# A shorter lead of the row maxima over the exponentials: 28 half-turns instead of 30

## The chip, the cores and the metric

The kernel runs on one core of a Trainium2 chip. Its time is device microseconds (us) for one execution; the times before are 1682.55, 1682.76 and 1683.22 us, median 1682.76. The engines are PE (the matrix multiplier, with its weight loads PEld), DVE (vector), ACT (scalar functions), POOL (general purpose) and SP, which here only issues DMAs. Each works through its own instructions strictly in the order in which they were written; they meet at semaphores.

## The reference

One transformer block with adaptive layer norm, 2048 tokens of width 512, 32 query heads of width 16 that share one key and one value head, and a bilinear gated layer of width 1792. Cut to what matters:

```python
mod = (_silu(c) @ w_mod).reshape(c.shape[0], 6, 1, -1)
sa, ca, ga, sb, cb, gb = (mod[:, 0], mod[:, 1], ..., mod[:, 5])
h = _layernorm(x) * (1 + ca) + sa
q, k, v = h @ wq, h @ wk, h @ wv                  # 32 heads of q, one of k and v
p = softmax(q @ k.T * 16 ** -0.5)                 # per head, 2048 x 2048
x = x + ga * ((p @ v) @ wo)
h = _layernorm(x) * (1 + cb) + sb
x = x + gb * (((h @ w_gate) * (h @ w_up)) @ w_down)
```

## The kernel before

**Units, turns, half-turns.** The tokens of q are cut in 4 blocks of 512, the heads in 8 groups of 4; a block with a group is a *unit*, 32 in all, and a unit has 16 *turns*, one for each 128 keys. For each turn PE computes four score tiles (tile `sc`, line 621, 128 keys by 512 queries), ACT takes their exponentials (tile `P`, line 623), and PE multiplies the exponentials of the turn before with the values (tile `pv`, line 632).

**Maxima.** The softmax needs the maximum of every score row first. So all scores are computed twice: once with queries on the partitions (tile `mx`, line 570), where DVE reduces each tile of 512 keys to its maximum (`mpart`, line 574), and once for the exponentials. A unit has 32 maxima steps (the first has 24), each with one tile in the upper half of PE's rows and one in the lower (`a` = 0 and 1). When the last step of a unit is done, DVE folds the partial maxima into `mm` (line 591). PE then transposes `mm` (tile `mxt`, line 598), ACT and DVE split the result into two half-precision rows (`mt`, lines 603 and 604), and two DMAs from SP put them into rows 48 and 49 of the query tile `sst` (line 608). The score matmul of that unit contracts over 50 rows, so it subtracts the maxima itself; it can start only when both DMAs have landed. Three `sst` tiles take turns.

**Order.** All instructions are written out by hand in program order; no scheduler moves them. First comes a *lead* of `LEAD` rounds, in which only maxima steps run, with the last of the preparation beside them: the modulation rows (`misc`, line 868, four matmuls for each of four rounds, then a copy and transposes) from round `M_STEP` on, and the first q product, in bursts of two or three matmuls (`Q_BURSTS`, tile `side`, line 485). After it, each turn writes two half-turns of maxima and two of exponentials, so the maxima stay `LEAD` half-turns ahead, until they run out.

**Side work.** Between them stands the work of the other layers (`side`, line 485): q products for later blocks (a store of q, line 518, goes out through SP), output projection, gate, up and down products. Two turns form an `attend`. With q products as side work its string is `FEW`, with the other products `MANY`, with none `NO_SIDE`. In `FEW` and `MANY` the maxima of the upper rows stand in the first turn and those of the lower rows in the second; `NO_SIDE` alternates.

**Where the row maxima are handed over.** A finished unit leaves its transposes under the step at which they may be written, one maxima step after the last. `late_max` looks for them in the middle of a turn and at its end. It writes the transposes and leaves the copies and DMAs for the next `drain_posts`, which stands at the start of a turn and in its middle, there just ahead of `late_max`:

```python
if last:
    max_fin(u)
    (_, f, g), = max_rows(u)
    later[mstep[1] + 1] = (f, g)      # f: transposes, g: copies and DMAs
...
drain_posts()
for j, (what, a) in enumerate(order):
    if j == len(order) // 2:
        drain_posts()
        late_max()
```

At the end of a unit the maxima's counter `mstep`, the exponentials and the lead thus decide together in which turn transposes, copies and DMAs fall.

Of the kernel before, what the change touches and what calls it, by code (L numbers as in the profile page):

```python
# [24 lines left out]
NU = NB * UB  # L25
KT = S // 128
FT = F // 128
LEAD = 30
WARM = (21, 3, 2, 3)
ABS_GAP = 2.5  # L30
SUM_GAP = 7.0
# [2 lines left out]
QPRE = 24  # L34
TR_WAIT = 11
NHF = 12
M_STEP = 23
PAIRED = 14
Q_BURSTS = {26: 3, 27: 3, 28: 3, 29: 2}

CHANNEL = {0: KC - 1, 3: 0, 4: 1, 6: 2}
LOW = -3.0e38
# [12 lines left out]
def adaln_mqa_glu_kernel(ctx: ExitStack, tc: tile.TileContext, x_in, wq_in, wk_in, wv_in, wo_in,  # L55
# [453 lines left out]
    def q_proj(b, ch):  # L509

        def evac(p):
            q16 = work.tile([128, 2, BT], F16, name="q16", tag="ev", bufs=3)
            qf = work.tile([128, BT], F32, name="qf", tag="ev", bufs=3)
            nc.scalar.activation(qf, p, AF.Copy, scale=qvs[:, 0:1])
            nc.gpsimd.tensor_scalar(q16[:, 0, :], qf, 1.0, 0.0, op0=OP.mult, op1=OP.add)
            nc.gpsimd.tensor_tensor(q16[:, 1, :], qf, q16[:, 0, :], op=OP.subtract)
            d = dram.tile([128, 2, BT], F16, name=f"qd{b}_{ch}")
            nc.sync.dma_start(d, q16)
            qd[b, ch] = d

        def op(i):
            k, term = divmod(i, 3)
            wl, hl = TERMS[term]
            return wq[:, wl, k, ch * 128:(ch + 1) * 128], h16[:, hl, k, b * BT:(b + 1) * BT]

        return Group(3 * KC, op, evac)
# [511 lines left out]
    def drain_posts():  # L1038
        todo = posts[:]
        posts.clear()  # L1040
        if tick[0] is not None:
            tick[0] += 1
            todo += timers.pop(tick[0], [])
        for f in todo:
            f()
# [56 lines left out]
    qs = deque(q_proj(b, ch) for b in range(NB) for ch in range(KC) if b + ch)  # L1102
    for n in range(LEAD):
        drain_posts()
# [5 lines left out]
        if n in first:  # L1110
            first[n]()
        for _ in range(Q_BURSTS.get(n, 0)):
            qs[0].whole()
        if 0 <= n - M_STEP < len(mod_rows):
            mod_rows[n - M_STEP]()
    cur.append(qs[0])
# [163 lines left out]
```

## Time and profile before

| what | value |
|---|---|
| median of 3 runs | 1682.76 us |
| profiled execution, its own time | 1682.67 us |
| span of that execution, first to last instruction | 1680.6 us |
| busy: PE, DVE, ACT, POOL | 1656.3, 1390.0, 1216.1, 518.1 us |
| lead, until the first score tile starts | 74.38 us |
| units 0 to 5, with q products beside them | 74.38 to 323.73 us |
| units 6 to 8, with no side work for most of the time | 323.73 to 446.54 us |
| units 11 to 30, output, gate, up and down products beside them | 539.35 to 1468.36 us |
| last unit, and the products that are left over | 1468.36 to 1680.6 us |

A line of the profile names the engine, the line of the code and the operation, then the tile written and, behind the arrow, the tiles read. In the rows of a stretch of time the first two numbers are start and length in us, "x4" says that four such instructions in a row are put together, and a bracket gives the idle time of the engine before it and who ended it. PE's times are modelled: matmuls follow each other every 0.21 us though each is shown with 0.38 us. SPq is the issue of a DMA, not its transfer.

### The profile page before, as it was taken

Reading aid. Unit: us, or ns where it says so; the run is one execution under the profiler, and the core shown is the slowest. Engines: PE = TensorE matmul, PEld = TensorE weight load, DVE = VectorE, ACT = ScalarE, POOL = GpSimd, SP = SyncE. Lnnn points to the kernel's source line nnn. Section 1 sums busy time; section 2 is a strip of 40 time slices with the busy share of each in tenths; the row PEclk is TensorE's granted clock in tenths of the full one; section 3 lists DMA queues with packets and bytes.
Section 4 is the critical chain, followed back from the end, with each engine's and each line's share of the span. In section 5 each row is a group of like instructions: output and inputs, shape, how many; then the busy total and the mean of one; then the engine's idle time right before and its main releaser. Section 6 shows DMA issues by size and latency. Waiting matters only on the chain.

```text
span 1680.6 us, 33352 instructions
## 1 busy us (share of the span) xinstructions
PE 1656.3 (99%) x12749; PEld 535.4 (32%) x12749; DVE 1390.0 (83%) x2365; ACT 1216.1 (72%) x2288; POOL 518.1 (31%) x690
## 2 busy tenths in 40 slices
PE   8999999999999999999999999999999999999999
PEld 3333333222223333333333333333333333334444
DVE  7999999999989999999989999999998999703110
ACT  5688888888787778777777777877777777772010
POOL 5745354626676740200140211101032111112230
PEclk9999999999999999999999999999999999999999
DMA  6112122211321200001100000000010000001000
GB/s 245 72 40 88 54 88 61 94 48 50 84 66 56 85 22 9 17 10 29 35 15 12 15 15 10 16 10 17 24 32 12 23 16 6 12 5 49 13 1 25
DMA packets 48556, 66.33 MB, mean 39 GB/s; under 512 B 14726, under 2 KB 29194, under 8 KB 48396
## 3 DMA queue, kind: packets, MB, share of 16 engines
q1 hardware_dynamic: 46812, 63.87, 12.2%
q8 instruction: 100, 1.64, 0.4%
q14 instruction: 60, 0.49, 0.1%
q10 hardware_dynamic: 1584, 0.33, 0.1%
HBM read 51.05 MB, written 8.65 MB: 36 GB/s over the span
## 4 chain that ended last, share of the span: by engine, by line
PE 87%; DVE 9%; ACT 2%; DMA 1%; issue 0%; ACTq 0%; DVEq 0%
PE side L485 50%; PE pv L632 27%; DVE mpart L574 8%; PE sc L621 5%; PE mx L570 3%; ACT P L623 2%; PE mx L765 1%; DMA xbig<-in_A_x_dram 1%; PE mxt L598 0%; DVE bs L238 0%; PE sc L570 0%; PE pk L274 0%; DMA wkv<-in_A_wv_dram 0%; DVE rel L579 0%; PE part L267 0%
## 5 line engine op out<-in xcount | busy, mean ns | idle before, releaser
L574 DVE TENSOR_REDUCE mpart<-mx 128x1 f32<-128x512 f32 x2016 | 1266.1, 683 | 91.6 <-PE mx L570 88.3
L623 ACT ACTIVATE P<-sc 128x512 f32<-128x512 f32 x2048 | 1092.0, 599 | 264.6 <-PE sc L621 223.1
L621 PE MATMUL sc<-sst,kst 50*128 50x512 f16 x2048 | 661.0, 379 | 1.0 <-DVE mpart L574 0.8
L570 PE MATMUL mx<-kst,sst 48*128 48x512 f16 x2032 | 617.3, 377 | 6.5 <-DVE mpart L574 3.8
L632 PE MATMUL pv<-P,vst 128*32 128x512 f32 x4096 | 545.3, 605 | 1.2
L485 PE MATMUL side<-h2T,wg 64*128 64x512 f16 (+1 forms) x1168 | 284.3, 378 | 0.1
L485 PE MATMUL side<-h2T,wu 64*128 64x512 f16 (+1 forms) x1166 | 282.9, 378 | 0.1
L485 PE MATMUL side<-wd,glu 64*128 64x512 f16 (+1 forms) x1008 | 234.1, 378 | 0.0
L818 POOL TENSOR_SCALAR glu<-gf 128x512 f16<-128x512 f32 x56 | 34.7, 620 | 617.2 <-DVE gf L817 538.9
L621 PEld LDWEIGHTS <-kst 50*128 50x128 f16 x2048 | 175.2, 94 | 129.4 <-issue 109.6
L570 PEld LDWEIGHTS <-sst 48*128 48x128 f16 x2064 | 183.9, 94 | 58.7 <-issue 37.4
L485 PEld LDWEIGHTS <-wg 64*128 64x128 f16 (+1 forms) x1168 | 100.9, 94 | 202.7 <-ACT P L623 95.0
L485 PEld LDWEIGHTS <-wu 64*128 64x128 f16 (+1 forms) x1166 | 100.8, 95 | 200.2 <-ACT P L623 92.5
L632 PEld LDWEIGHTS pv<-P,vst 128*32 128x32 f32 x4096 | 80.8, 108 | 218.8 <-issue 202.8
L485 PEld LDWEIGHTS <-glu 64*128 64x128 f16 (+1 forms) x1008 | 89.1, 95 | 163.2 <-ACT P L623 63.0
L817 DVE TENSOR_TENSOR gf<-side,g 128x512 f32<-128x512 f32 x56 | 38.3, 684 | 115.8 <-PE side L485 82.5
L485 PE MATMUL side<-h,wq 64*128 64x512 f16 (+1 forms) x349 | 92.5, 376 | 0.0
L812 ACT ACTIVATE g<-side 128x512 f32<-128x512 f32 x56 | 33.2, 593 | 81.5 <-PE side L485 81.5
L485 PE MATMUL side<-wo,och 64*128 64x512 f16 (+1 forms) x336 | 79.3, 378 | 0.0
L819 POOL TENSOR_TENSOR glu<-gf,glu 128x512 f16<-128x512 f32 x56 | 65.0, 1161 | 4.7
L200 POOL TENSOR_SCALAR rv<-st 128x1 f32<-128x1 f32 (+1 forms) x20 | 4.6, 228 | 158.3 <-DVE st L725 143.2
L666 POOL TENSOR_TENSOR oc<-oc,rr 128x512 f32<-128x512 f32 x15 | 19.1, 1275 | 107.4 <-DMA sst<-qd 94.3
(223 smaller groups left out, 810.5 us busy)
## 6 DMA issues: line engine op xcount, KB each, us to landing
wsl<-in_B_w_gate_dram SPq DMA_DIRECT2D x32, 224.0 KB
wsl<-in_B_w_up_dram SPq DMA_DIRECT2D x32, 224.0 KB
wsl<-in_B_w_down_dram SPq DMA_DIRECT2D x28, 256.0 KB
sst<-qd SPq DMA_DIRECT2D x180, 32.0 KB
oc<-ev SPq DMA_DIRECT2D x128, 32.0 KB
rr<-ri SPq DMA_DIRECT2D x16, 256.0 KB
xl<-in_A_x_dram SPq DMA_DIRECT2D x16, 256.0 KB
qd<-q SPq DMA_DIRECT2D x15, 256.0 KB
```

What stands on the lines that cost most here:

```text
L485: return nc.tensor.matmul(self.p, left[64 * r0:64 * r1], right[64 * r0:64 * r1], start=start, stop=self.ended())
L570: nc.tensor.matmul(m, s[64 * a:64 * a + 48, p, t * 128:(t + 1) * 128], w[64 * a:64 * a + 48, :], start=(i == 0), stop=(i == len(keys) - 1))
L574: nc.vector.tensor_reduce(part, m, axis=AX.X, op=OP.max)
L621: nc.tensor.matmul(t, kst[64 * a:64 * a + 50, kt * 128:(kt + 1) * 128], s[64 * a:64 * a + 50, p, :], start=True, stop=True)
L623: ex = nc.scalar.activation(ptl[u, kt, p, a], t, AF.Exp)
L632: nc.tensor.matmul(pvb[u][32 * j:32 * j + 32, :], vst[:, kt, :], ptl[u, kt, p, a], start=(kt == 0), stop=(kt == KT - 1))
L666: eng.tensor_tensor(o, o, st["r"], op=OP.mult)
L765: nc.tensor.transpose(st["p"][:, t * 128:(t + 1) * 128], n2s[b, t][:, k * 128:(k + 1) * 128], ident)
L812: nc.scalar.activation(st["g", f], p, AF.Copy, scale=2.0 ** -45)
L817: nc.vector.tensor_tensor(gf, p, st["g", f], op=OP.mult)
L818: nc.gpsimd.tensor_scalar(st["glu"][:, 0, f, :], gf, 1.0, 0.0, op0=OP.mult, op1=OP.add)
L819: nc.gpsimd.tensor_tensor(st["glu"][:, 1, f, :], gf, st["glu"][:, 0, f, :], op=OP.subtract)
```

## The change

Three numbers: the lead has 28 rounds; the modulation rows start in round 21 and the bursts of the first q product in round 24, so that both end with the lead as before. No instruction's work is changed.

```diff
-LEAD = 30
+LEAD = 28
 ...
-M_STEP = 23
+M_STEP = 21
 PAIRED = 14
-Q_BURSTS = {26: 3, 27: 3, 28: 3, 29: 2}
+Q_BURSTS = {24: 3, 25: 3, 26: 3, 27: 2}
```

From round 14 on a round of the lead is one maxima step. So four `mx` tiles of unit 1 leave the lead, every later maxima step stands two half-turns later against the exponentials, and the last ones of unit 31 stand where side work stood.

The first place is ACT at the beginning of unit 16. `mt` is the first copy of the row maxima, `P` the exponentials (of unit 15 ahead of `mt`), `ev` the copy of unit 15's result, which marks the second turn of unit 16. Before:

```order
L623 ACTIVATE P<-sc 128x512 x8
L812 ACTIVATE g<-side 128x512
L623 ACTIVATE P<-sc 128x512 x40
L603 ACTIVATE mt_11690<-mxt 16x128
L623 ACTIVATE P<-sc 128x512 x16
L638 ACTIVATE ev<-pv,evs 128x512
```

After, at the same place:

```order
L623 ACTIVATE P<-sc 128x512 x8
L812 ACTIVATE g<-side 128x512
L623 ACTIVATE P<-sc 128x512 x48
L603 ACTIVATE mt_11758<-mxt 16x128
L623 ACTIVATE P<-sc 128x512 x8
L638 ACTIVATE ev<-pv,evs 128x512
```

The first copy moves behind eight more exponentials: of the 16 that stood between it and `ev`, eight were unit 15's last two turns; now unit 16's own follow it at once. It is so in 27 of the units 1 to 31. In four (6, 7, 8 and 10, which begin without side work) it moves behind four, and one turn of the old unit is left between.

The second place is SP ahead of unit 2. `qd` is a store of q, `wsl` a load of a weight slice, `sst<-mt` the two rows of maxima. Before:

```order
L897 DMA wsl<-in_B_w_gate_dram 128x448 x3
L608 DMA sst_128<-mt_2213 2x8x128
L608 DMA sst_128<-mt_2214 2x8x128
L897 DMA wsl<-in_B_w_gate_dram 128x448
L518 DMA qd_2_2297<-q_2292 128x1024
L897 DMA wsl<-in_B_w_gate_dram 128x448
```

After:

```order
L518 DMA qd_1_2029<-q_2024 128x1024
L897 DMA wsl<-in_B_w_gate_dram 128x448
L535 DMA sst_126<-qd_1_1039 16x2x512 x6
L897 DMA wsl<-in_B_w_gate_dram 128x448 x3
L518 DMA qd_2_2279<-q_2274 128x1024
L608 DMA sst_128<-mt_2285 2x8x128
L608 DMA sst_128<-mt_2286 2x8x128
```

The rows of maxima moved behind a load and behind the store of q. The same happens ahead of unit 5.

The third place is PE in the lead, at the first of the modulation rows. `mx` and `sc` from line 570 are maxima steps of unit 0 (sst_126) and unit 1 (sst_127). Before:

```order
L570 MATMUL mx<-kst,sst_126 128x512
L868 MATMUL misc<-wmB,silr 32x512 x2
L868 MATMUL misc<-wmA,silr 32x512
L868 MATMUL misc<-wmB,silr 32x512
L570 LDWEIGHTS sst_127
L570 MATMUL mx<-kst,sst_127 128x512
```

After:

```order
L868 MATMUL misc<-wmB,silr 32x512 x2
L868 MATMUL misc<-wmA,silr 32x512
L868 MATMUL misc<-wmB,silr 32x512
L570 LDWEIGHTS sst_126
L570 MATMUL mx<-kst,sst_126 128x512
L570 LDWEIGHTS sst_126
L570 MATMUL sc<-kwb,sst_126 128x512
L570 LDWEIGHTS sst_126
L570 MATMUL sc<-kst,sst_126 128x512
```

The first two groups of modulation matmuls now stand among unit 0's last maxima steps, which have three matmuls for each half; before, all four stood behind them.

## Prediction, made before the changed kernel was run

> **What bounds the kernel now.** I read the page's busy shares and its chain of waits first, then busy time by stretch, then single rows at the end of a unit.
>
> ```profile
> PE 1656.3 (99%) x12749; PEld 535.4 (32%) x12749; DVE 1390.0 (83%) x2365; ACT 1216.1 (72%) x2288; POOL 518.1 (31%) x690
> PE 87%; DVE 9%; ACT 2%; DMA 1%; issue 0%; ACTq 0%; DVEq 0%
> 158.13:323.73 165.60, 164.42 (x1309) 50.01 (x1307) 160.85 (x274) 140.49 (x274) 83.57 (x84) 1.00 0.24 75
> 323.73:446.54 122.81, 116.34 (x855) 30.23 (x852) 121.78 (x219) 102.25 (x199) 61.31 (x79) 1.00 0.20 59
> 539.35:1468.36 929.01, 928.03 (x7703) 286.69 (x7700) 844.75 (x1386) 730.38 (x1363) 179.58 (x215) 1.00 0.07 20
> ```
>
> The stretches give length, then busy PE, PEld, DVE, ACT, POOL, then the granted clock. PE is never idle for long in the units with gate, up and down products (928.03 of 929.01 us), PE and DVE nearly together limit those with q products, DVE (121.78 of 122.81) those without side work. So whatever stops PE between units is lost: in the first kind PE has no slack, and in the others DVE's next maxima stand behind the same scores in PE's order. The execution profiled took 1682.67 us (span 1680.6), 0.09 under the median; I add to 1682.67.
>
> **The hand-over of the row maxima.** Here is the start of unit 16 before; its first score tile starts at 769.87.
>
> ```profile
> 763.20 0.22 DVE L591 TENSOR_REDUCE mm<-mpart 128x16 f32<-128x64 f32 x1
> 763.99 0.28 PE L598 MATMUL mxt<-ident,mm 128*16 128x128 f32 x1
> 764.30 0.27 ACT L603 ACTIVATE mt<-mxt 16x128 f16<-16x128 f32 x1 [0.52 <-PE mxt L598]
> 764.60 0.28 DVE L604 SCALAR_TENSOR_TENSOR mt<-mxt,mt 16x128 f16<-16x128 f32 x1
> 764.59 1.22 SPq L608 DMA_DIRECT2D sst<-mt  x2
> 767.03 0.39 PE L621 MATMUL sc<-sst,kst 50*128 50x512 f16 x1
> 767.46 2.19 ACT L623 ACTIVATE P<-sc 128x512 f32<-128x512 f32 x4 [0.64 <-PE sc L621]
> 767.68 2.56 DVE L574 TENSOR_REDUCE mpart<-mx 128x1 f32<-128x512 f32 x4 [0.30 <-PE mx L570]
> 769.87 0.39 PE L621 MATMUL sc<-sst,kst 50*128 50x512 f16 x1
> 770.38 2.08 ACT L623 ACTIVATE P<-sc 128x512 f32<-128x512 f32 x4 [0.73 <-PE sc L621]
> ```
>
> A turn is 2.84 us (767.03 to 769.87). The second DMA has been issued by 765.81, 4.06 us ahead of the score, and the score waits for nothing. With a lead of 28 the last maxima step of the lower rows falls on the last place of its turn instead of the second. The transposes are allowed one step later; in `FEW` and `MANY` the next turn holds steps of the upper rows alone, so they come in the middle of the turn after that, the old unit's last, and the copies at the very start of the new unit, just ahead of its scores. The order of ACT above shows it. What was two turns ahead is now none.
>
> How long PE then stands, in times from the first score's place s = 769.87: ACT finishes the old unit's exponentials at 767.46 + 2.19 = s − 0.22 and the first copy at s + 0.05; its DMA occupies SP to s + 0.7. DVE finishes the reductions queued ahead at 767.68 + 2.56 = s + 0.37 and the second copy at s + 0.65. Both paths let SP issue the second DMA at about s + 0.7. Its landing is not shown by a row of its own; the nearest rows are DMAs whose reader waits on SP:
>
> ```profile
> L608 SPq DMA_DIRECT2D sst<-mt x64: 508/544/652, 68.1 to 1463.7; - x64
> L647 SPq DMA_DIRECT2D rs<-ev x32: 528/550/555, 124.7 to 1517.9; - x32
> SPq L654 <- DMA rs<-ev: 12.4, 12, 1.2
> L659 SPq DMA_DIRECT2D ri<-rc x16: 325/326/344, 215.1 to 1521.8; - x16
> SPq L661 <- DMA ri<-rc: 18.3, 16, 2.0
> ```
>
> Issue plus mean wait is 0.55 + 12.4/12 = 1.58 us for 8 KB and 0.33 + 18.3/16 = 1.47 for 16 KB. The first has the same issue time as ours (0.54), so I take 1.6; the ends are 1.4 and 2.3 (0.33 + the longest wait). The score starts at s + 0.7 + 1.6: **a wait of 2.3 us** where there was none, between 2.0 and 3.0. The transposes' own 0.2 us of PE only move from one turn to another.
>
> Counted from ACT's order, 27 of 31 hand-overs are of this kind: 27 × 2.3 = 62.1 us. Unit 31 has no maxima beside it, so its second copy comes earlier, but the first DMA's issue still holds SP to s + 0.7; I leave it at 2.3. Something more stands ahead of the copies in several:
>
> ```profile
> 110.32 0.71 ACT L514 ACTIVATE qf<-side,qvs 128x512 f32<-128x512 f32 x1
> 111.14 0.27 ACT L603 ACTIVATE mt<-mxt 16x128 f16<-16x128 f32 x1
> 113.00 0.34 SPq L518 DMA_DIRECT2D qd<-q  x1
> 113.44 1.15 SPq L608 DMA_DIRECT2D sst<-mt  x2
> 154.35 0.34 SPq L897 DMA_DIRECT2D wsl<-in_B_w_gate_dram  x1
> 158.13 0.39 PE L621 MATMUL sc<-sst,kst 50*128 50x512 f16 x1
> 160.31 0.33 SPq L518 DMA_DIRECT2D qd<-q  x1
> 283.99 0.39 PE L621 MATMUL sc<-sst,kst 50*128 50x512 f16 x1
> 285.98 0.35 SPq L518 DMA_DIRECT2D qd<-q  x1
> L812 ACT ACTIVATE g<-side 128x512 f32<-128x512 f32 x56 | 33.2, 593 | 81.5 <-PE side L485 81.5
> L817 DVE TENSOR_TENSOR gf<-side,g 128x512 f32<-128x512 f32 x56 | 38.3, 684 | 115.8 <-PE side L485 82.5
> ```
>
> Ahead of unit 1 the row was copied by 111.41 and its DMA left only at 113.44, behind a store of q that waited for POOL: SP's order counts. Before units 2 and 5 that store now stands ahead of the DMAs, and it is ready only 2.2 and 2.0 us after their scores' old place. Two issues (1.2) and 1.6 us after its own 0.3 they land at s + 5.1: 2.8 us more, twice, 5.6. In units 13, 21, 24 and 29 ACT has one more copy of a side tile ahead (line 812, 0.6 each), in 17 and 27 DVE one more result of the size of line 817's (0.7 each): 3.8. The weight load that moved ahead of unit 2's rows was issued at 154.35, 3.8 us before s, and costs nothing; the single loads and stores that moved ahead elsewhere were issued over 1.4 us before the score too, but for an output store of unit 27, whose result is counted. In the four hand-overs without side work (6, 7, 8, 10) one turn of some 2.4 us remains: the same chain ends about 0.1 to 0.3 after s, with DVE still behind PE; I take 0.6 for the four, between 0 and 2. Sum of the waits: 62.1 + 5.6 + 3.8 + 0.6 = **72.1 us**.
>
> **The lead.** Two rounds with four reductions leave it.
>
> ```profile
> 67.27 2.47 DVE L574 TENSOR_REDUCE mpart<-mx 128x1 f32<-128x512 f32 x4
> 68.02 0.62 PE L868 MATMUL misc<-wmB,silr 128*32 128x512 f32 x2
> 70.09 0.62 PE L868 MATMUL misc<-wmB,silr 128*32 128x512 f32 x2
> 74.38 0.39 PE L621 MATMUL sc<-sst,kst 50*128 50x512 f16 x1
> ```
>
> Four reductions are 2.47 us of DVE: the most the lead can gain. But PE is the limit where modulation rows and bursts meet, 2.07 us a round (68.02 to 70.09), and all of these stay; two groups now meet three matmuls a half instead of one and push PE past DVE there (1.6 us a round against 1.2 by the spacing of the rows, 0.4 each). And unit 0's rows lose the two rounds that covered their landing. I take −1.3, between −2.5 and +0.5. The modulation weights have landed by then (the share of DMA, the last number but one, is 0.00 in the stretch from 50.19 below), so starting sooner waits for nothing. At the end four half-height maxima tiles stand where side tiles stood, which follow later as two whole matmuls: +0.4. Without an effect on the clock: 1682.67 + 72.1 − 1.3 + 0.4 = 1753.9 us.
>
> **The clock.** PE's granted clock fell once within the work:
>
> ```profile
> 42.20 1.12 PE L274 MATMUL pk<-part,selk 128*128 128x512 f32 x2 [1.38 <-ACT part L269]
> 54.80 0.58 PE L570 MATMUL sc<-kst,sst 48*128 48x512 f16 x1 [2.06 <-DVE kst L289]
> 50.19:53.60 3.41, 2.54 (x17) 1.28 (x16) 3.35 (x7) 2.43 (x5) 3.24 (x5) 1.00 0.00 0
> 53.60:57.01 3.41, 2.21 (x12) 0.96 (x13) 3.41 (x6) 1.31 (x3) 3.24 (x5) 0.50 0.00 0
> 57.01:60.43 3.42, 3.42 (x20) 1.62 (x18) 3.42 (x12) 2.84 (x6) 3.25 (x5) 0.50 0.00 0
> ```
>
> The wait that ended at 54.80, the longest of PE after its start, was followed by half the clock for 6.83 us, which is two stretches of 3.41; waits up to 1.38 kept it. The new waits of 2.3 us and more are longer than the one that lost it, so I expect some of them to lose it too, by how they lie on a grid of 3.41 us. I take half of 27, 14. Each then runs a stretch of 3.41 at half speed where PE is the limit: 1.5 us lost, 21 in all, so **1775 us**. The ends are none (1754) and all, with both stretches lost as in the row (27 × 3.2 = 86, 1840).
>
> [...]
>
> **The rivals.**
> - Waits without the clock: 1745 to 1760, likeliest 1754. For it: units without side work, where DVE holds PE up in every turn, kept 1.00. Against: the row at 53.60. Chance 0.27.
> - Both stretches lost after most waits: over 1800. For it: the one case seen did so. Against: its first stretch still held 1.2 us of that wait, ours hold less. Chance 0.08.
> - The waits partly absorbed: only units where PE is the limit pay (22 × 2.3 less 1), or PE's turn, which has 2.69 us of work in its 2.84 (eight pairs of 0.213 and 0.99 of `pv` by the spacing of starts), catches up some of it: 1690 to 1745. Against: PE and DVE both stand idle behind the score. Chance 0.08.
> - Not slower: the rows still land before the score. It decides at a chain of 2.3 us that would have to start one turn sooner, as it does where there is no side work; then the waits fall to about 0 and 1682.67 − 1.3 + 0.4 = 1681.8 is left, no change that a measurement of this kernel can tell (that bound is 0.2%, 3.4 us); even the whole 2.5 us of the lead would not pass it. Against: ACT's order puts the copy right ahead of unit 16's own exponentials. Chance 0.03.
>
> **How the numbers follow.** Waits with some clock lost, 1760 to 1800, has 0.54 and gives 1775. The range 1745 to 1800 takes in this and the first rival, 0.81 in all, and so the ends of the landing time (27 × −0.3 to +0.7). Faster 0.01, within the bound 0.03, slower 0.96.
>
> **What would show it.** In the new profile the first score tile of a unit has an idle PE of 2 to 2.5 us ahead of it, ended by the DMA of the rows, some 5 us for units 2 and 5, and next to none for 6, 7, 8 and 10. The rows' copies stand within 1 us of it. The lead ends at about 73 us. The mean granted clock falls from 0.998 to about 0.985 (14 × 3.41 at half of 1775) if the clock falls at half of the hand-overs. I would be wrong if the DMA landed much sooner than 1.6 us after issue, or if the clock went after every wait or after none.

## The result, and the profile after

The changed kernel takes 1775.59 us, median of four runs (1773.6 to 1777.47), against 1682.66 for the kernel before (four runs, 1682.55 to 1683.22). The ratio is 1.0549, with an interval of 1.0537 to 1.0561: slower by 93 us, where 92 were forecast. The profiled execution took 1773.6 us with a span of 1771.8.

From the page after: the busy shares, the chain of waits, and the group of the score tiles (busy time, mean ns, idle time before them):

```profile
PE 1688.7 (95%) x12747; PEld 539.7 (30%) x12747; DVE 1392.5 (79%) x2365; ACT 1214.8 (69%) x2288; POOL 518.0 (29%) x690
PE 84%; DVE 9%; ACT 3%; DMA 3%; issue 1%; SPq 1%; POOL 0%; ACTq 0%
L621 PE MATMUL sc<-sst,kst 50*128 50x512 f16 x2048 | 667.7, 382 | 61.4 <-DMA sst<-mt 60.0
```

From the list of waits after (us in total, times, longest):

```profile
PE sc L621 <- DMA sst<-mt: 60.0, 28, 4.8
```

And the span with the mean granted clock:

```profile
core 0: 1771.8 us, clock 0.985
```

PE's share falls from 99% to 95%. Its idle time has one name: the score tiles of line 621 waited 60.0 us, in 28 pieces, for the DMAs that bring the row maxima. DVE, ACT and POOL do the same work as before, to within 3 us. PE's busy time grew by 32.4 us although its work did not: its matmuls ran slower for some of the time (eight `pv` take 1.06 us at the end of unit 15 and 1.94 behind unit 16's hand-over, in rows below), as the mean clock shows, which fell from 0.998 to 0.985, and PE's modelled ends run on into the waits.

By stretch of time after (start and end, length, busy PE, PEld, DVE, ACT, POOL, granted clock, DMA share, GB/s), for the units 0 to 5, 6 to 8, and 11 to 30:

```profile
73.48:342.29 268.81, 251.65 (x1969) 76.76 (x1970) 243.25 (x412) 210.87 (x410) 123.03 (x125) 0.98 0.22 67
342.29:467.48 125.19, 116.57 (x851) 30.39 (x851) 122.20 (x218) 102.11 (x198) 61.43 (x84) 1.00 0.21 61
563.89:1559.17 995.28, 953.72 (x7700) 288.83 (x7701) 847.68 (x1389) 729.30 (x1363) 177.15 (x213) 0.98 0.07 19
```

The first stretch grew by 19.5 us (249.35 before), the second by 2.4 (122.81), most of it at the end of unit 8, which is the wait ahead of unit 9, where side work begins again; the third by 66.3 (929.01). The lead ends at 73.48 instead of 74.38. From there to the last score tile it is 1529.76 us instead of 1438.06 (+91.7), and what follows that is 0.4 longer.

The start of unit 16 again, from the timeline after:

```profile
808.27 1.06 PE L632 MATMUL pv<-P,vst 128*32 128x512 f32 x8
808.41 0.60 ACT L623 ACTIVATE P<-sc 128x512 f32<-128x512 f32 x1 [0.25 <-PE sc L621]
808.90 0.25 ACT L603 ACTIVATE mt<-mxt 16x128 f16<-16x128 f32 x1
809.18 1.22 SPq L608 DMA_DIRECT2D sst<-mt  x2
809.54 0.27 DVE L604 SCALAR_TENSOR_TENSOR mt<-mxt,mt 16x128 f16<-16x128 f32 x1
811.51 0.39 PE L621 MATMUL sc<-sst,kst 50*128 50x512 f16 x1 [1.86 <-DMA sst<-mt]
813.37 1.94 PE L632 MATMUL pv<-P,vst 128*32 128x512 f32 x8
```

The stretches of the four turns around it, from one `pv` to the next, and behind them two stretches of the clock:

```profile
805.12:808.27 3.15, 3.15 (x27) 0.87 (x25) 2.60 (x5) 2.39 (x5) 0.00 (x0) 1.00 0.00 0
808.27:813.37 5.10, 3.24 (x24) 0.93 (x22) 2.75 (x6) 2.12 (x5) 0.00 (x0) 0.99 0.02 5
813.37:817.97 4.60, 4.48 (x26) 1.09 (x25) 2.76 (x6) 2.50 (x6) 0.00 (x0) 0.64 0.00 0
817.97:820.80 2.83, 2.83 (x24) 0.88 (x24) 2.83 (x5) 2.43 (x5) 0.00 (x0) 1.00 0.04 16
...
809.87:813.27 3.40, 1.75 (x13) 0.68 (x13) 1.11 (x2) 1.27 (x3) 0.00 (x0) 1.00 0.01 2
813.27:816.68 3.41, 3.41 (x17) 0.79 (x18) 1.79 (x4) 1.46 (x3) 0.00 (x0) 0.50 0.00 0
```

The order is as forecast: the last exponential of unit 15 ends at 809.01, the first copy at 809.15, the second at 809.81, its DMA is issued behind it, and the score starts at 811.51. Two costs stand next to each other. The turn with the hand-over takes 5.10 us instead of 2.84, which is 2.27 more by the exact starts (the idle time shown, 1.86, is smaller, since PE's ends are modelled and its shown work runs on for some 0.4 us into the wait). The next turn takes 4.60, because the clock is at 0.50 from 813.27 for one stretch of 3.41 us.

### The profile page after: what moved, and what is told of

The parts are those of the page before. It is cut to its first block, busy times and chain, and to the rows that moved or that the text cites. A ratio compares the mean times of both kernels' runs of the same rounds, so it can differ in the third digit from the quotient of the medians.

```text
span 1771.8 us, 33297 instructions
## 1 busy us (share of the span) xinstructions
PE 1688.7 (95%) x12747; PEld 539.7 (30%) x12747; DVE 1392.5 (79%) x2365; ACT 1214.8 (69%) x2288; POOL 518.0 (29%) x690
## 4 chain that ended last, share of the span: by engine, by line
PE 84%; DVE 9%; ACT 3%; DMA 3%; issue 1%; SPq 1%; POOL 0%; ACTq 0%
PE side L485 46%; PE pv L632 25%; DVE mpart L574 8%; PE sc L621 6%; PE mx L570 4%; DMA sst<-mt 3%; ACT P L623 2%; PE misc L159 1%; SPq L608 1%; PE mx L765 0%; PE sc L570 0%; PE mxt L598 0%; PE part L267 0%; PE pk L274 0%; PE misc L868 0%
## 5 line engine op out<-in xcount | busy, mean ns | idle before, releaser
L621 PE MATMUL sc<-sst,kst 50*128 50x512 f16 x2048 | 667.7, 382 | 61.4 <-DMA sst<-mt 60.0
L570 PE MATMUL mx<-kst,sst 48*128 48x512 f16 x2032 | 624.2, 381 | 6.9 <-DVE mpart L574 4.0
L632 PE MATMUL pv<-P,vst 128*32 128x512 f32 x4096 | 554.9, 614 | 1.1
L485 PE MATMUL side<-h2T,wg 64*128 64x512 f16 (+1 forms) x1168 | 289.1, 381 | 0.0
```

The source lines that it names most:

```text
L485: return nc.tensor.matmul(self.p, left[64 * r0:64 * r1], right[64 * r0:64 * r1], start=start, stop=self.ended())
L570: nc.tensor.matmul(m, s[64 * a:64 * a + 48, p, t * 128:(t + 1) * 128], w[64 * a:64 * a + 48, :], start=(i == 0), stop=(i == len(keys) - 1))
L621: nc.tensor.matmul(t, kst[64 * a:64 * a + 50, kt * 128:(kt + 1) * 128], s[64 * a:64 * a + 50, p, :], start=True, stop=True)
L632: nc.tensor.matmul(pvb[u][32 * j:32 * j + 32, :], vst[:, kt, :], ptl[u, kt, p, a], start=(kt == 0), stop=(kt == KT - 1))
```

## The experiments

Each edit is against the changed kernel unless another is named. All leave the computation as it is; two add matmuls whose results nobody reads.

### One half-turn less than before: 29

```diff
-LEAD = 28
+LEAD = 29
-M_STEP = 21
+M_STEP = 22
-Q_BURSTS = {24: 3, 25: 3, 26: 3, 27: 2}
+Q_BURSTS = {25: 3, 26: 3, 27: 3, 28: 2}
```

> The lead is 29, the modulation rows start in round 22 and the bursts in round 25. Theory (grid of turns): the cost comes from the turn in which the copies of the row maxima are written, and with 29 the last maxima step of the lower rows still leaves the transposes to the end of its own turn, so the copies stay two turns ahead of the scores, as with 30. Then no score waits for the rows' DMAs, the clock stays at 1.00 after the lead, and the time is 1682 to 1690 us: half of the lead's gain, less some tenths of a us a unit in which the transposes wait for DVE. Rival (in proportion): every half-turn of lead that is given up costs half of the 93 us, so 29 gives some 1729 us.

Measured: 1684.13 us over 10 runs, against 1682.73; ratio 1.0007 (0.9997 to 1.0016). No first score of a unit waits, and the mean clock is 0.998. The loss is thus not in proportion to the lead: one half-turn costs nothing that can be measured, the second 91 us. What decides is the turn in which the hand-over is written.

### Two half-turns fewer still: 26

```diff
-LEAD = 28
+LEAD = 26
-M_STEP = 21
+M_STEP = 19
-Q_BURSTS = {24: 3, 25: 3, 26: 3, 27: 2}
+Q_BURSTS = {22: 3, 23: 3, 24: 3, 25: 2}
```

> The lead is 26, modulation rows from round 19, bursts from round 22. Theory (grid of turns): the copies are again written at the very start of the new unit, as with 28; only the transposes come later, at the end of the old unit's last turn, and the units without side work lose their one turn too. So each wait grows by some 0.3 us and four waits of 2.5 us are added: 1785 to 1800 us with the clock falling as often or a little more. Rival (in proportion): two more half-turns cost 93 us more, some 1868 us.

Measured: 1814.75 us, two runs (1810.52 and 1818.97), ratio 1.0783 (1.076 to 1.0807). That is above the range expected and far under what a rise in proportion would give. From its list of waits:

```profile
PE sc L621 <- DMA sst<-mt: 84.9, 32, 5.9
```

The first score of unit 0 in its timeline:

```profile
76.38 0.58 PE L621 MATMUL sc<-sst,kst 50*128 50x512 f16 x1 [2.74 <-DMA sst<-mt]
```

And stretches at the end of its lead and in unit 0:

```profile
75.00:78.41 3.41, 2.04 (x9) 0.86 (x11) 1.22 (x2) 1.19 (x3) 0.00 (x0) 0.50 0.44 132
78.41:81.83 3.42, 3.42 (x18) 1.22 (x18) 3.26 (x7) 2.61 (x6) 0.00 (x0) 0.50 0.01 2
81.83:85.24 3.41, 3.41 (x18) 0.67 (x12) 1.57 (x3) 2.18 (x4) 2.11 (x3) 0.50 0.00 0
```

The waits stand where the order says: units 6 to 8, which began with next to none at 28, now wait 2.4 to 2.5 us, and unit 0 waits for its own rows (2.74). Two sizes were too small. The waits shown grew by 24.9 us (84.9 instead of 60.0), where 0.3 us for each of 27 and four of 2.5 would have made some 18: unit 16's went from 1.86 to 2.35, and unit 9's from 1.79 to 5.89, since the rows' DMAs stood behind a weight load that itself waited for POOL (issued at 485.06, the rows at 485.48; their second copy was done at 482.24). And the clock was lost more often. In the profiled execution it is at half for 102.4 us, where it was 54.6 at 28 (6.8 of it in the preparation, here 10.2), and three stretches in a row are lost around the start of unit 0. The waits alone do not say how often the clock falls.

### The hand-over one turn sooner, all else as changed

The transposes are allowed by the count of all maxima steps, upper and lower, instead of the lower ones, so that they are written in the middle of the turn before.

```diff
-            later[mstep[1] + 1] = (f, g)
+            later[sum(mstep) + 1] = (f, g)
...
-        for at in [m for m in later if m <= mstep[1]]:
+        for at in [m for m in later if m <= sum(mstep)]:
```

> The lead of 28 with all its moves stays; only the test by which a finished unit's transposes are let through counts the maxima steps of both halves instead of the lower rows' alone, so that they come in the middle of the next turn and the copies one whole turn (2.8 us) ahead of the scores. Theory (the wait for the rows' DMAs is the whole loss, the clock included): the chain of 2.3 us ends before the scores, the mean granted clock is back at 0.998, and the time is 1682 to 1688 us, the lead's gain of about 0.9 us nearly used up at the end and by small waits. Rival (the changed order itself, the later maxima or the lead's moves cost something): well over 1690 us, with the waits gone and the time not back.

Measured: 1685.58 us over 11 runs, ratio 1.0016 (1.0007 to 1.0025). The waits of the first scores are gone (0.5 us are left), and so is the loss of clock:

```profile
core 0: 1683.4 us, clock 0.998
```

Its stretch with the units 11 to 30:

```profile
538.47:1470.80 932.33, 931.16 (x7706) 285.11 (x7702) 846.28 (x1390) 728.78 (x1363) 179.34 (x215) 1.00 0.07 20
```

The lead still has 28 rounds and the bursts stand where the change put them, so 90 of the 93 us are the place of the hand-over alone. That stretch is 3.3 us longer than before (929.01), and PE has no more idle time in it. In the changed kernel the turn with the transposes in its middle took 3.15 us (805.12 to 808.27), before, with the transposes at a turn's end, 3.04. A tenth a unit accounts for about 2 of the 3.3 us; the last experiment tests it.

### The early modulation and q product, at a lead of 30

```diff
-LEAD = 28
+LEAD = 30
```

> The other part of the change alone: the lead stays at 30 rounds, the modulation rows start in round 21 and the bursts in round 24. Theory: these moves cost and bring next to nothing, 1681 to 1684 us, no waits for the rows, granted clock 0.998. Rival: they have a part of their own in the 93 us.

Measured: 1684.7 us over 11 runs, ratio 1.0012 (1.0003 to 1.0021), just above what was expected. The lead ends at 72.95, 1.4 us sooner, and the gain is lost again in unit 0, which takes 45.41 us instead of 42.23. Stretches of its start:

```profile
74.57:77.98 3.41, 2.37 (x12) 0.63 (x12) 3.41 (x7) 2.17 (x4) 0.00 (x0) 1.00 0.69 219
77.98:81.39 3.41, 3.41 (x17) 0.43 (x15) 2.69 (x5) 1.99 (x4) 0.62 (x1) 0.50 0.00 0
```

And one of the waits in its timeline:

```profile
74.74 0.37 PE L621 MATMUL sc<-sst,kst 50*128 50x512 f16 x1 [0.23 <-DVE mpart L574]
```

With the bursts gone from the lead's last rounds, PE has less to do there (2.37 us of 3.41, while DVE is busy throughout) and waits for DVE in small pieces. No single wait in that stretch is longer than a few tenths, and still the clock is at half for the next 3.41 us. This part of the change, done alone, is no gain.

### The clock held through the waits: ten idle matmuls

In units with side work beside them, ten matmuls that no one reads are written before the first score, where PE would wait. At 0.21 us each they fit into an ordinary wait of 2.3 us.

```diff
             drain_posts()
+            if kt + turn == 0 and u > 0 and style is not NO_SIDE:
+                pw = ps_mx("fillup")
+                for _ in range(10):
+                    nc.tensor.matmul(pw, kst[:, 0:128], kst[:, 0:512], start=True, stop=True)
```

> The changed kernel (lead 28) with ten idle matmuls of 512 columns, whose result nobody reads, written on PE ahead of the first score of each unit that begins with side work beside it; they take about 2.1 us of PE, nearly the length of the wait. Theory (waits of 2.3 us and, on top, half the clock after about half of them): the matmuls fill the wait without making it longer, the clock stays at 1.00 but perhaps after the two long waits, mean 0.996 or more, and the time falls by some 20 us to 1750 to 1759 us. Rival (the clock's falls cost nothing, since another engine is the limit in those stretches): the clock is mended and the time stays within 4 us of 1775, or grows by the matmuls.

Measured: 1758.18 us over 4 runs, ratio 1.0445 (1.0429 to 1.0461), in the range expected. The group of the idle matmuls in its page of groups:

```profile
L1152 PE MATMUL fillup<-kst 128*128 128x512 f16 x270 | 62.9, 380 | 0.0
```

Its list of waits:

```profile
PE sc L621 <- DMA sst<-mt: 6.1, 4, 2.5
```

And its clock:

```profile
core 0: 1757.4 us, clock 0.995
```

The scores start no sooner, as the 75.5 us of loss that remain (below) show; only the idle time has become busy time. What the kernel gains by this, 1775.59 − 1758.18 = 17.4 us, is the clock's part of the loss. After the lead the clock falls only twice, at 166.4 and 302.93, in units 2 and 5, whose waits are longer than ten matmuls (one stretch of the preparation, from 43.52, is lost besides). The rest, 1758.18 − 1682.7 = 75.5 us, is the waits' own part with what these two falls still cost.

### Four idle matmuls

```diff
-                for _ in range(10):
+                for _ in range(4):
```

(against the kernel with ten)

> As the one with ten idle matmuls, but with four: about 0.85 us of the wait of 2.2 filled, 1.3 us left idle. Theory (the clock falls when a stretch of 3.41 us has less than some four tenths of its time with matmuls streaming): 1.3 us of idle time leave every stretch above that but at the two or three long waits, so nearly all of the gain of the ten is kept, 1750 to 1762 us, mean clock 0.994 or more. Rival (any wait after which matmuls stop for about 1.3 us can lose the clock): some four to eight falls stay and the time lies between, near 1765 us.

Measured: 1759.07 us over 4 runs, ratio 1.0449 (1.0432 to 1.0466). From its list of waits:

```profile
PE sc L621 <- DMA sst<-mt: 35.0, 28, 3.8
```

Two stretches around unit 27's hand-over:

```profile
1346.70:1350.11 3.41, 1.16 (x11) 0.47 (x12) 0.31 (x1) 0.47 (x1) 0.00 (x0) 1.00 0.23 84
1350.11:1353.52 3.41, 3.41 (x17) 0.52 (x13) 2.27 (x4) 1.70 (x4) 0.00 (x0) 0.50 0.00 0
```

About 1 us of most waits is idle again, 35.0 in 28, and yet nearly all the clock is kept: after the lead it falls in units 2 and 5 and once more, at 1350.11, at the longer wait of unit 27. The gain over the changed kernel is 16.5 us, nearly that of ten. So four matmuls ahead of the score, 0.85 us at 0.21 each, kept the clock at all but three of the 27 hand-overs here. That the clock falls when matmuls stream for less than some four tenths of a stretch was my estimate, and no run shows such a limit: in the changed kernel the stretch from 960.04, with PE shown busy for 1.96 of 3.41 us, was followed by half clock, and the one from 1557.37, with 1.62, was not.

### The sooner hand-over without the transposes in the middle of a turn

Against the kernel with the sooner hand-over: where side work stands beside a unit, the transposes wait for the end of the turn.

```diff
                 if j == len(order) // 2:
                     drain_posts()
-                    late_max()
+                    if style is NO_SIDE:
+                        late_max()
```

> As the kernel that counts both halves' maxima steps, but beside side work the transposes wait for the end of that turn instead of its middle; the copies stay at the start of the old unit's last turn, 2.84 us ahead of the scores (2.5 where q products run). Theory (the chain alone decides, counted from the transposes): the copy on ACT now waits for the transposes, so the chain is some 0.5 us longer, the DMA lands 2.8 to 3.0 us after the turn's start, and a wait of 0 to 0.2 us is left at most hand-overs, 0.2 to 0.6 where q products run; the clock is kept, the time is 1682 to 1690 us. Rival (what matters is only whether a turn stands between copies and scores): no wait at all, and the time lower than with the transposes in the middle by the 0.1 us a unit that they cost there.

Measured: 1683.61 us over 10 runs, against 1682.86; ratio 1.0004 (0.9994 to 1.0014). Its clock is 0.998. In its list of waits the loads of the scores' weights stand with the rows of maxima, 6.0 us in 8 pieces:

```profile
PEld L621 <- DMA sst<-mt: 6.0, 8, 1.1
```

It is 2.0 us faster than the kernel with the transposes in the middle, which is what a tenth a unit makes, and its stretch with the units 11 to 30 takes 930.35 us instead of 932.33. Of these waits only 0.1 to 0.3 us reach PE, in six units: I had looked for more. It equals the kernel before within what can be measured. No version of this study is clearly faster than that kernel.

## Why the prediction was right

**The place of the hand-over.** It stands as forecast: the copies fall within 1 us of the scores' old place. (The list of signs had them within 1 us of the first score tile; as that tile now waits, the second copy ends 1.70 us ahead of it in unit 16, 809.81 to 811.51.) The sooner hand-over at the same lead takes 90 of the 93 us back. The rivals with a gain or with no change assumed rows that land in time; the same rows, written a turn sooner, did.

**2.3 us for each of 27.** At unit 16 the turn grew by 2.27. The list of waits shows 1.80 to 1.87 for an ordinary hand-over, and read by that row alone the forecast would seem a fifth too high; the spacing of the turns is the measure. The landing, taken as 1.6 us from the second issue, gave a score at 0.7 + 1.6 after its old place; it was 1.70 from the end of the second copy. Waits, lead and end together were put at 71.2 us without the clock; the kernel with ten idle matmuls shows 75.5, by estimate some 72.5 without its two falls at 1.5 each. The rival of waits partly absorbed falls with that: by the two experiments that hold the clock, the kernel without the clock's part is at 1755 to 1759, not under 1745.

**What stands ahead of the copies.** These rows are from the timeline after: SP and PE in unit 2, then PE in units 5 and 27:

```profile
161.29 0.33 SPq L518 DMA_DIRECT2D qd<-q  x1
161.71 1.22 SPq L608 DMA_DIRECT2D sst<-mt  x2
164.14 0.58 PE L621 MATMUL sc<-sst,kst 50*128 50x512 f16 x1 [4.79 <-DMA sst<-mt]
300.81 0.39 PE L621 MATMUL sc<-sst,kst 50*128 50x512 f16 x1 [4.57 <-DMA sst<-mt]
1361.86 0.39 PE L621 MATMUL sc<-sst,kst 50*128 50x512 f16 x1 [3.22 <-DMA sst<-mt]
```

The store of q goes first on SP and the rows follow it; against the ordinary 1.86 the two waits are 2.9 and 2.7 us longer (2.8 forecast). Units 13, 21, 24 and 29 wait 2.35 to 2.40, half a microsecond more, for the extra copy of a side tile (0.6 forecast). Unit 17 waits 0.4 more (0.7 forecast), and so does unit 23, for which nothing was forecast.

Unit 27 waits 1.4 more (0.7 forecast). There the prediction counted the result of DVE that delays the second copy, but the output store of that result also stands ahead of the rows on SP: DVE is done with it at 1359.05, the store is issued at 1359.08 and the two rows only behind it, from 1359.53, although the first copy had ended at 1358.10. In unit 16 the issue follows the first copy by 0.03 us, here by 1.43, and that is the whole 1.4.

Of the four hand-overs without side work two wait 0.11 and two nothing (0.6 together, forecast).

**The lead and the end.** The lead gained 0.9 instead of 1.3; of the 0.4 that is missing, 0.28 is unit 0's first score waiting for its rows. The end cost 0.4, as forecast.

**The clock.** Fourteen stretches of 3.41 us at half clock were forecast after the lead, and the profiled execution has fourteen, in 13 falls; only in unit 2 are both stretches lost. So close a match is luck. That the share is a half was a choice between none and all, and no row of the profile before could have given it; with two half-turns fewer, 27 stretches are lost from the lead's end on. The other three runs of the changed kernel were slower, at mean clocks of 0.982 to 0.984 instead of 0.985, and by that lost up to three stretches more (an estimate: 0.003 of 1776 us at half clock is 10.7 us). Nor was the wait of 1.38 in the preparation, which had kept the clock, a safe one: the same wait, 1.37 us, is followed by half clock in both kernels with idle matmuls (from 43.52 and 42.80).

The price stands better. From its first score to the next unit's, unit 16 takes 50.78 us in the changed kernel and 49.22 with ten idle matmuls; the eleven units that lose one stretch in the first and none in the second differ by 1.35 to 1.63 us, about 1.5 as forecast.

The falls lie on a grid, as assumed: those at 714.28 and 813.27 are 29 times 3.413 us apart. The stretches ahead of them were not idle: ten of the 13 falls stand behind waits shown as 1.79 to 2.40 us, the stretch ahead of the fall at 813.27 holds 13 matmuls and one wait of 1.86, and even the emptiest, 297.85 to 301.27, holds six matmuls. The rival of waits without the clock, 1754, is what the kernel costs where the clock is held (1758), and not what it costs.

## What to carry to other kernels

How far ahead a value is handed over counts in the turns of the written order, not in proportion: one half-turn less was free, the next put the copies on ACT and DVE one block of work later and cost 91 us, and writing them one turn sooner gave 90 back. Where PE must wait some 2 us, price the clock beside the wait, here about 1.5 us for every second one, and read the wait from the spacing of the turns rather than from the idle time shown. Where the wait stayed, four or ten matmuls that nobody reads kept most of the clock here, worth 17 us.

## What the runs showed of the hardware that was not expected

In the profile after, each of the 13 falls of the clock behind the lead, from 161.32 to 1461.80, begins a whole number of steps of 3.413 us after the fall in the preparation at 55.51 (31 steps for the first, 412 for the last), and 12 of them lasted one stretch of 3.41. None of the stretches ahead of these falls was idle: PE is shown busy in them for 0.46 us (from 297.85) to 1.96 us (from 960.04) of 3.41. That time alone does not sort them: the stretches from 1557.37, with 1.62, and from 1007.83, with 1.77, kept the clock, and the one from 809.87, with 1.75, was followed by half clock. What sorts them, these runs leave open.

Three measured cases stand beside this. Half clock followed a wait shown as 1.79 us (unit 9, the fall at 468.52). Where four matmuls stood in waits like it, the clock fell three times after the lead instead of 13. And with the early modulation and q product at a lead of 30, the stretch from 74.57 at the start of unit 0 was followed by half clock although the waits listed in it are 0.20 to 0.23 us each, with PE shown busy for 2.37 us of 3.41.
